# Linear attention and channel mix on one core: q turned in blocks on VectorE, the attention weights moved by DMA, and an order from a table

## The chip, the core and the metric

The kernel runs on one core of one Trainium2 chip. TensorE (PE) multiplies matrices, VectorE (DVE), ScalarE (ACT) and GpSimd (POOL) do elementwise work, and SyncE (SP), ACT and POOL issue DMA transfers. The metric is the device time of one execution in microseconds, the median of several.

## What is computed

Inputs in float32: q, k and v of (8 batches, 8 heads, 576 rows, 64), and the weights of a feed-forward part. The reference, cut to what matters:

```python
def _attn_ref(q, k, v):
    q_s = softmax(q, over the 64 columns)
    k_s = softmax(k, over the 576 rows)
    kv = einsum('bhsd,bhse->bhde', k_s, v)
    return einsum('bhsd,bhde->bhse', q_s, kv)

def _moe_ref(x, mu_k, mu_r, w_k, w_v, w_r):      # x: (8, 576, 512), heads side by side
    x_prev = x shifted by one row, zeros first
    xk = mu_k * x + (1.0 - mu_k) * x_prev
    xr = mu_r * x + (1.0 - mu_r) * x_prev
    k = np.maximum(xk @ w_k, 0.0)                # (512, 1024)
    v = k * k @ w_v                              # (1024, 512)
    r = 1.0 / (1.0 + np.exp(-(xr @ w_r)))        # (512, 512)
    return r * v
```

There is no softmax over a square matrix: each head's k and v give a 64 x 64 matrix kv, and q is multiplied by it.

## The kernel before

**Attention.** `attention(b, g)` handles four heads of one batch: g is 0 or 1. Their q, k and v are loaded as float32 into `raw` buffers of 128 partitions: a partition holds nine rows of a head, and two heads lie one above the other. ACT takes the exponent of q and of k to bfloat16 (`eq`, `ek`, L423) and casts v (`vv`, L430). DVE sums q's rows (`rsum`, L437), inverts the sums (L440) and scales (`qs`, L445). PE transposes `qs` against an identity in nine 128 x 128 blocks into the PSUM tile `att` (L472), and ACT copies the result to `qt` (L476). PE forms kv in 18 products on 64 rows each (L453), one column of ones in `vv` giving the sums over k's rows as well. DVE inverts these (`rz`, L460) and scales kv into block-diagonal weights `w` (L560). PE multiplies them with `qt` (x, L566), ACT copies the product to `xb` (L571), and DVE mixes each row with the row before: `edge` (L575), `diff` (L579), a product with mu (L584) and a sum (L589) into `xk` and `xr`, which hold four batches. Batch 0 goes another way: its weights are multiplied with mu beforehand (`mu_mask`, L513), so that PE does the mixing as well (L525), and its results are copied to `xk` and `xr` (L530).

**Channel mix.** `unit(half, c0, n)` handles 512 or 256 columns of `xk` and `xr`: eight groups of four products with `wk_bf` (L646), a relu on ACT (`rel`, L631), a square on DVE (`k2`, L635); then, per 128 rows, four products with `wr_bf` (L677), a tanh on ACT (L682), eight products with `wv_bf` (L687), the gate on DVE (`ot`, L693) and two stores of 128 KB on SP's queue (L703).

**Order.** Every step is entered with `plan.add`, with its engine, an assumed duration, what it depends on and which buffers it takes. `Plan.order` then plays the program through: `set_due` gives each step a due time, counted back from the channel mix, and of the steps that could start on an engine the one with the least due time is taken. `early` and `AHEAD` shift due times. The result is a fixed order for each engine; an engine executes its own strictly in that order. `pools` gives the number of buffers of each kind. The tiles `mm` (four of one PSUM bank) and `att` (two of two banks) fill PSUM.

**Loads.** Batch 0's q, k and v come in halves on ACT's and SP's queues (`FIRST`). All else goes by POOL's queue: the weights, cast to bfloat16 by the transfer, in the order wk, wr, wv, with batch 1's loads between and behind (`SOON`), then the batches 2 to 7. The first weight load waits for one of batch 0's loads (`GATE`).

Of the kernel before, what the change touches and what calls it, by code (L numbers as in the profile page):

```python
# [19 lines left out]
SPARE = 0  # L20
LOOK = {"PE": 0.03, "ACT": 0.2, "DVE": 0.1, "POOL": 0.03, "SP": 0.03}
AHEAD = (1.0, 4, 8)
# [8 lines left out]
         (0, 2, ("SP", "SP")), (1, 1, ("SP", "SP")), (1, 2, ("SP", "SP")))  # L31
ORDER = (0, 1, 2)
SOON = {(1, 0, 0): 2.2, (1, 0, 1): 2.4, (1, 1, 0): 2.7, (1, 0, 2): 3.5}
GATE = 6
FILL = 0
ON_PE = (0,)
CASTS = (("ACT", "ACT"), ("ACT", "ACT"))
EVAC = ((("ACT", "DVE"), ("ACT", "ACT")), (("ACT", "DVE"), ("ACT", "ACT")))

# [10 lines left out]
class Op:  # L50


    def __init__(self, engine, occ, lat, key, emit, deps, takes, gives, size):
        self.engine, self.occ, self.lat, self.key = engine, occ, lat, key
        self.emit, self.deps, self.takes, self.size = emit, list(deps), list(takes), size
        self.start = self.end = None
        self.early = 0.0
        for slot in gives:
            slot.last.append(self)


class Plan:
# [11 lines left out]
    def add(self, engine, occ, lat, key, emit, deps=(), takes=(), gives=(), size=0.0):  # L74
        op = Op(engine, occ, lat, key, emit, [d for d in deps if d is not None], takes, gives,
                size)
        self.ops.append(op)
        return op

    def slot_time(self, slot):  # L80
        best = None
        for i, parts in enumerate(self.pools[slot.pool]):
            free = 0.0
            for user in (self.user.get(part) for part in parts):
                if user is not None:
                    late = [o.end for o in user.last]
                    free = None if not late or None in late or free is None else max(
                        [free] + late)
            if free is not None and (best is None or free < best[0]):
                best = (free, i)  # L90
        return best
# [9 lines left out]
    def set_due(self):  # L101
        after = {}
        for op in self.ops:
            for d in op.deps:
                after.setdefault(d, []).append(op)
        seen = set()
        for root in self.ops:
            stack = [(root, False)]
            while stack:
                op, closed = stack.pop()  # L110
                if closed and not op.size:
                    for o in after.get(op, ()):
                        op.key = min(op.key, o.key - op.lat - HOP - SPARE)
                    op.key -= op.early
                elif op not in seen:
                    seen.add(op)
                    stack.append((op, True))
                    stack += [(o, False) for o in after.get(op, ())]

    def order(self):  # L120
        self.set_due()
# [3 lines left out]
        waiting = {}  # L125
        for op in self.ops:
            waiting.setdefault(op.engine, []).append(op)
        done = []
        left = len(self.ops)
        while left:  # L130
            chosen = None
            for engine, ops in waiting.items():
                now = free.get(engine, START)
                ready = None
                for op in ops:
                    if any(d.end is None for d in op.deps):
                        continue
                    t = max([now] + [d.end + HOP for d in op.deps])
                    ok = True
                    for slot in op.takes:  # L140
                        got = self.slot_time(slot)
                        if got is None:
                            ok = False
                            break
                        t = max(t, got[0] + HOP)
                    if not ok:
                        continue
                    rank = (max(t, now + LOOK[engine]), op.key)
                    if ready is None or rank < ready[0]:
                        ready = (rank, t, op)  # L150
                if ready is not None and (chosen is None or ready[1] < chosen[1]):
                    chosen = ready
            assert chosen is not None, "no operation can start"
            _, t, op = chosen
            for slot in op.takes:
                slot.index = self.slot_time(slot)[1]
                for part in self.pools[slot.pool][slot.index]:
                    self.user[part] = slot
# [12 lines left out]
            waiting[op.engine].remove(op)  # L171
            done.append(op)
            left -= 1
        return sorted(done, key=lambda o: o.start)
# [3 lines left out]
def kernel(  # L178
# [25 lines left out]
    pools = {"raw": 12, "eq": 3, "ek": 2, "vv": 2, "stat": 4, "qs": 2, "qt": 3, "w": 3, "wp": 4,  # L204
             "rz": 3, "xb": 2, "xd": 2, "xm": 3, "k2": 2, "rel": 3, "th": 2, "ot": 3, "mm": 4,
             "att": 2, "early": 2}
    shared = {("early", i): [("mm", 2 * i), ("mm", 2 * i + 1)] for i in range(2)}
    plan = Plan(pools, shared)
# [17 lines left out]
    ws = buffers("w", [128, 2, 128], BF16)  # L226
    wps = buffers("wp", [128, 2, 2, 128], BF16)
    rzs = buffers("rz", [128, 2], F32)
    xbs = buffers("xb", [128, 2, 64 + S], BF16)
    xds = buffers("xd", [128, 2, S], BF16)  # L230
    xms = buffers("xm", [128, 2, S], BF16)
    k2s = buffers("k2", [128, FT, 512], BF16)
    rels = buffers("rel", [128, 512], BF16)
# [14 lines left out]
    wk_bf = const.tile([128, CT, F], BF16, name="wk_bf")  # L248
# [9 lines left out]
    mu_mask = const.tile([128, 2, 2, CT, 128], F32, name="mu_mask")  # L258
# [6 lines left out]

    def load(engines, b, g, i, key, deps=()):
        slot = Slot("raw")
        src = (q, k, v)[i]
        us = PARTS[len(engines)]

        def emit(engine, u):
            ap = bass.AP(tensor=src.tensor,
                         offset=src.offset + (b * H + 2 * g + 4 * u.start) * S * D,
                         ap=[[J * D, 128], [4 * S * D, u.stop - u.start], [1, J * D]])
            return queues[engine].dma_start(out=raws[slot.index][:, u, :], in_=ap)

        ops = [plan.add(e, 0.71 if e == "POOL" else 0.45, 0.5, key + 0.1 * n,
                        lambda e=e, u=u: emit(e, u), deps, [slot] if n == 0 else [],
                        size=590.0 / len(engines))
               for n, (e, u) in enumerate(zip(engines, us))]  # L280
        loaded[b, g, i] = (ops, slot)
        return ops

    first = []
    for n, (g, i, engines) in enumerate(FIRST):
        first += load(engines, 0, g, i, n)

# [20 lines left out]

    def emit_mask_zeros():
        nc.vector.memset(mu_mask[:].rearrange("p m s c e -> p (m s c e)"), 0.0)  # L310

    def emit_late_consts():
        for t in ws:
            nc.vector.memset(t[:].rearrange("p a b -> p (a b)"), 0.0)
        for t in xbs:
            nc.vector.memset(t[:, :, 0:1], 0.0)

# [4 lines left out]
    consts = plan.add("DVE", 0.2, 0.3, -9, emit_consts, [identity])  # L322
    late_consts = plan.add("DVE", 0.6, 0.7, LATE, emit_late_consts)
    mask_zeros = plan.add("DVE", 1.8, 1.9, 0, emit_mask_zeros)
# [47 lines left out]
    def weight_part(dst, src, n, u, c0, c1):  # L372
        ap = bass.AP(tensor=src.tensor, offset=src.offset + (4 * u + c0) * D * n,
                     ap=[[n, 64], [D * n, c1 - c0], [1, n]])
        return nc.gpsimd.dma_start(out=dst[64 * u:64 * u + 64, c0:c1, :], in_=ap)

    gate = [first[GATE]]
    sync = mybir.DependencyInfo(mybir.DependencyClass.Sync, mybir.DependencyReason.DATA)

    def emit_wk(h):  # L380
        for u in range(2):
            ld = weight_part(wk_bf, moe_w_k, F, u, 2 * h, 2 * h + 2)
            if h == u == 0:
                tc.add_manual_dep(ld.ins, gate[0].made.ins.name, sync)

    wk_done, wv_done = [], []
    for h in range(2):
        wk_done.append(plan.add(
            "POOL", 1.25, 1.25, h, lambda h=h: emit_wk(h), gate, size=1048.0))
    wr_done = plan.add("POOL", 1.25, 1.25, 2, lambda: [  # L390
        weight_part(wr_bf, moe_w_r, C, u, 0, CT) for u in range(2)], gate, size=1048.0)

    def emit_wv(h):
# [3 lines left out]
        nc.gpsimd.dma_start(out=wv_bf[:, h * n:(h + 1) * n, :], in_=ap)  # L397

    for h in range(2):
        wv_done.append(plan.add("POOL", 0.75, 0.75, 3 + h, lambda h=h: emit_wv(h), gate,  # L400
                                size=1048.0))
    for b in range(1, B):
        for g in range(2):
            for n, i in enumerate(ORDER):
                load(["POOL"] * (2 if b == 1 else 1), b, g, i,
                     SOON.get((b, g, i), 100 * b + 10 * g + n), gate)
# [6 lines left out]
    def attention(b, g):  # L413
# [14 lines left out]
        def cast_v(copy, u):  # L428
            to = vvs[vv.index][:, :, 0:128].rearrange("p j (u d) -> p j u d", u=2)
# [340 lines left out]
```

## Time and profile before

| what | us |
|---|---|
| three executions | 211.36, 211.47, 212.88 |
| median | 211.47 |
| span of the profiled execution | 210.3 |
| PE, DVE, ACT, POOL busy in it | 192.2, 160.3, 150.9, 43.2 |
| moved by DMA in it | 40.62 MB |

The profile is of one execution. A line such as `L646 PE MATMUL mm_c<-xk,wk_bf` names the kernel's line, the engine, the operation, and the tile written with the tiles read. In an answer on waits a line reads: who waited, for whom, microseconds in all, times, the longest. In the chain of waits a line has the start, the microseconds and the work. For transfers, a line has the target and source, the issuing queue, their number, the size of each and the median time in us from issue to landing. The bytes counted are those written, so a weight load that casts counts half of what it reads.

### The profile page before, as it was taken

The page shows a single profiled execution, that of the slowest core. Times are in us where ns is not written, and L with a number is a line of the kernel's source. Part 1 is how long each engine was busy: PE and PEld are TensorE (multiplying, and loading weights), DVE is VectorE, ACT ScalarE, POOL GpSimd, SP SyncE. Part 2 cuts the span into 40 slices and gives each one's busy share as a digit, 9 for nine tenths or more (in the row PEclk, how much of TensorE's full clock was granted, in tenths as well). Part 3 has the DMA queues.
Part 4 walks back from the last instruction along what each step waited for, and adds up shares of the span by engine and source line. Part 5 has one row for each costly group of instructions (what it writes and reads, how often), then busy time and mean ns, then how long its engine had stood idle before and what let it go on. Part 6 is the DMA issues. An engine that isn't in the chain of part 4 may idle for free.

```text
span 210.3 us, 3597 instructions
## 1 busy us (share of the span) xinstructions
PE 192.2 (91%) x1283; PEld 97.2 (46%) x1283; DVE 160.3 (76%) x364; ACT 150.9 (72%) x229; POOL 43.2 (21%) x72
## 2 busy tenths in 40 slices
PE   3089998967999999999999999999999999999991
PEld 0065444433544544445467444445444554444740
DVE  6488684999999999999959995957796469632531
ACT  5596798998999999759599977338964862452440
POOL 3793656534334132301100000000000000000000
PEclk9999999999999999999999999999999999999999
DMA  6999999999999999983871130350034003502424
GB/s 216 367 215 201 346 267 394 392 405 403 392 395 404 404 383 339 317 277 112 245 196 41 31 69 0 71 119 14 6 86 111 2 3 85 115 0 50 102 51 100
DMA packets 15898, 40.62 MB, mean 193 GB/s; under 512 B 2300, under 2 KB 3848, under 8 KB 15880
## 3 DMA queue, kind: packets, MB, share of 16 engines
q0 software_dynamic: 8384, 27.40, 39.7%
q1 hardware_dynamic: 7064, 12.10, 20.4%
q10 hardware_dynamic: 432, 0.88, 1.3%
q8 instruction: 10, 0.16, 0.3%
q14 instruction: 8, 0.07, 0.1%
HBM read 33.56 MB, written 9.44 MB: 204 GB/s over the span
## 4 chain that ended last, share of the span: by engine, by line
PE 82%; DVE 7%; ACT 4%; DMA 3%; issue 1%; ACTq 0%; DVEq 0%
PE mm_b L646 9%; PE mm_c L646 8%; PE mm_a L687 7%; PE mm_d L687 7%; PE mm_b L687 7%; PE mm_a L646 6%; PE mm_c L687 6%; PE mm_d L677 5%; PE mm_d L646 5%; PE mm_c L677 4%; DMA raw_b<-in_k_dram 3%; PE mm_a L677 2%; PE att_a L472 2%; PE att_a L453 2%; PE att_b L453 2%; PE att_b L472 2%
## 5 line engine op out<-in xcount | busy, mean ns | idle before, releaser
L646 PEld LDWEIGHTS <-wk_bf 128*128 128x128 bf16 x320 | 30.4, 98 | 31.0 <-issue 2.3
L646 PE MATMUL mm_b<-xk,wk_bf 128*128 128x512 bf16 (+1 forms) x96 | 23.2, 357 | 0.0
L646 PE MATMUL mm_c<-xk,wk_bf 128*128 128x512 bf16 (+1 forms) x92 | 22.6, 361 | 0.0
L677 PEld LDWEIGHTS <-xr 128*128 128x128 bf16 x144 | 13.4, 98 | 16.0 <-issue 0.7
L687 PEld LDWEIGHTS <-k_a 128*128 128x128 bf16 x144 | 13.5, 98 | 15.8 <-issue 0.5
L687 PEld LDWEIGHTS <-k_b 128*128 128x128 bf16 x144 | 13.4, 98 | 15.7
L646 PE MATMUL mm_a<-xk,wk_bf 128*128 128x512 bf16 (+1 forms) x72 | 17.1, 355 | 0.0
L646 PE MATMUL mm_d<-xk,wk_bf 128*128 128x512 bf16 (+1 forms) x60 | 14.9, 358 | 1.6 <-DVE xk L589 1.6
L677 PE MATMUL mm_d<-wr_bf,xr 128*128 128x512 bf16 x56 | 14.4, 379 | 0.0
L687 PE MATMUL mm_a<-wv_bf,k_a 128*128 128x512 bf16 x48 | 12.3, 379 | 0.0
L682 ACT ACTIVATE th_a<-mm_d 128x512 f32<-128x512 f32 x12 | 7.2, 602 | 6.8 <-PE mm_d L677 6.6
L677 PE MATMUL mm_c<-wr_bf,xr 128*128 128x512 bf16 x40 | 10.3, 379 | 0.1
L687 PE MATMUL mm_d<-wv_bf,k_a 128*128 128x512 bf16 x40 | 10.3, 379 | 0.0
L687 PE MATMUL mm_c<-wv_bf,k_b 128*128 128x512 bf16 x40 | 10.3, 379 | 0.0
L687 PE MATMUL mm_b<-wv_bf,k_b 128*128 128x512 bf16 x40 | 10.1, 379 | 0.0
L472 PEld LDWEIGHTS <-qs_a 128*128 128x128 bf16 x72 | 4.9, 103 | 8.6 <-DVE qs_a L445 7.4
L635 DVE TENSOR_TENSOR k_a<-rel_a 128x512 bf16<-128x512 bf16 (+1 forms) x13 | 5.1, 391 | 4.6 <-ACT rel_a L631 4.5
L631 ACT ACTIVATE rel_a<-mm_b 128x512 bf16<-128x512 f32 (+1 forms) x10 | 5.4, 539 | 4.0 <-PE mm_b L646 3.8
L687 PE MATMUL mm_a<-wv_bf,k_b 128*128 128x512 bf16 x32 | 8.2, 379 | 0.0
L687 PE MATMUL mm_d<-wv_bf,k_b 128*128 128x512 bf16 x32 | 8.2, 379 | 0.0
L687 PE MATMUL mm_c<-wv_bf,k_a 128*128 128x512 bf16 x32 | 8.2, 379 | 0.0
L682 ACT ACTIVATE th_b<-mm_a 128x512 f32<-128x512 f32 x6 | 3.6, 594 | 6.3 <-PE mm_a L677 6.3
(258 smaller groups left out, 452.5 us busy)
## 6 DMA issues: line engine op xcount, KB each, us to landing
out_dram<-ot_a SPq DMA_DIRECT2D x24, 128.0 KB, 2.7
out_dram<-ot_b SPq DMA_DIRECT2D x24, 128.0 KB, 2.4
out_dram<-ot_c SPq DMA_DIRECT2D x24, 128.0 KB, 2.7
raw_a<-in_q_dram POOLq DMA_DIRECT2D x3, 576.0 KB, 10.3
raw_c<-in_k_dram POOLq DMA_DIRECT2D x2, 576.0 KB, 10.3
raw_b<-in_v_dram POOLq DMA_DIRECT2D x2, 576.0 KB, 10.5
raw_d<-in_q_dram POOLq DMA_DIRECT2D x2, 576.0 KB, 10.2
raw_e<-in_k_dram POOLq DMA_DIRECT2D x2, 576.0 KB, 10.9
```

What stands on the lines that cost most here:

```text
L453: nc.tensor.matmul(kv_of(kvp, hf)[:, 0:129], lhsT=eks[ek.index][r, j, :, :].rearrange("p u d -> p (u d)"), rhs=vvs[vv.index][r, j, 0:129], ...
L472: nc.tensor.transpose(out=transposed()[:, j, :], in_=qss[qs.index][:, j, :], identity=ident[:])
L631: nc.scalar.activation(out=rels[rel.index][:, 0:n], in_=bank(kf)[:, 0:n], func=ACT.Relu, scale=HALF_ROOT)
L635: nc.vector.tensor_tensor(out=k2s[k2.index][:, fc, 0:n], in0=rels[rel.index][:, 0:n], in1=rels[rel.index][:, 0:n], op=ALU.mult)
L646: nc.tensor.matmul(bank(kf)[:, 0:n], lhsT=wk_bf[:, ct, fc * 128:(fc + 1) * 128], rhs=xs[0][:, ct, c0:c0 + n], start=(ct == 0), stop=(ct == ...
L677: nc.tensor.matmul(bank(rps), lhsT=xs[1][:, ct, c:c + 128], rhs=wr_bf[:, ct, :], start=(ct == 0), stop=(ct == CT - 1))
L682: nc.scalar.activation(out=ths[th.index][:], in_=bank(rps), func=ACT.Tanh, scale=0.5)
L687: nc.tensor.matmul(bank(vps), lhsT=k2s[k2.index][:, ft, 128 * m:128 * m + 128], rhs=wv_bf[:, ft, :], start=(ft == 0), stop=(ft == FT - 1))
```

## The change

Six things change.

1. Batches 2 to 7 go through a new function, `batch(b)`, which handles all eight heads at once. q is loaded in another layout (two transfers of 64 partitions for four heads), its exponent, sums and scaling are as before, and `turn_q` then transposes it on DVE in blocks of 32 x 32, taking two bfloat16 as one 4-byte element; PE's transposes and ACT's copies of them are gone. Since an element is a pair of columns, the 64 columns of a head come apart into 32 pairs: k's exponent writes its columns in the same order, and x is the sum of two products, r = 0 and 1.
2. kv of both groups goes into one `att` tile. Its inverse sums and weights are formed once per batch, without the block-diagonal zeros (`wn`), and four transfers on SP's queue move them from SBUF to SBUF into `w`, where each head has its 32 partitions.
3. x then is sixteen products per half batch, on tiles of 32 rows and 64 columns, 288 moving columns each, into two `att` tiles.
4. Batch 0's v is cast by its load, on POOL's queue, into the first `k2` buffer; its ACT casts are gone. `mu_mask` lies in the other `k2` buffer.
5. `wk_bf` becomes two tiles by columns, and the loads' order changes: batch 1's k and v, then parts of wk, q, wr and wv. `held` lets the first of POOL's gated loads wait, whichever it is.
6. The order is no longer found by due times: `ORDER_OF` lists all steps. `early`, `AHEAD` and `set_due` are gone. Some pools grow (`ek`, `vv`, `xb` to 3, `qt` and `rel` to 4).

The stores of batches 2 to 7 write rows in the new order. The core of the diff:

```diff
 FIRST = ((0, 0, ("ACT", "ACT")), (1, 0, ("SP", "SP")), (0, 1, ("ACT", "SP")),
-         (0, 2, ("SP", "SP")), (1, 1, ("SP", "SP")), (1, 2, ("SP", "SP")))
+         (1, 1, ("SP", "SP")), (0, 2, ("POOL",)), (1, 2, ("POOL",)))
...
-GATE = 6
+GATE = 5
...
+ORDER_OF = (
+    0, 20, 8, 16, 1, 10, 17, 13, 11, 3, 12, 6, 5, 2, 4, 14, 9, 15, 7, 21, 78, 79, 22, 80, 24, 81,
...
     def order(self):
-        self.set_due()
...
+        for i in ORDER_OF:
+            op = self.ops[i]
...
+    def batch(b):
...
+            def turn_q(qs=qs, qt=qt):
+
+                nc.vector.transpose(
+                    out=qts[qt.index][:].rearrange("p j c -> p (j c)").bitcast(F32),
+                    in_=qss[qs.index][:].rearrange("p j c -> p (j c)").bitcast(F32))
...
+                for y in range(u.start, u.stop):
+                    nc.scalar.activation(
+                        out=eks[ek.index][:].rearrange("p j u d -> p j (u d)").rearrange(
+                            "p j (r y d) -> p j y d r", r=2, y=2)[:, :, y, :, :],
+                        in_=raws[sk.index][:, y, :].rearrange("p (j d r) -> p j d r", d=32, r=2),
+                        func=ACT.Exp)
...
+        def kv():
+            for g in range(2):
+                for j in range(J):
+                    for x in range(2):
+                        r = slice(64 * x, 64 * x + 64)
+                        nc.tensor.matmul(
+                            bank(kvp)[:, x, 256 * g:256 * g + 129],
+                            lhsT=eks[eks_[g].index][r, j, :, :].rearrange("p u d -> p (u d)"),
+                            rhs=vvs[vvs_[g].index][r, j, 0:129], start=(j == 0),
+                            stop=(j == J - 1), skip_group_check=True)
...
+        def weights(x):
+            nc.vector.tensor_tensor(
+                out=wns[wn.index][:, x, :, :], in0=by_group(0, 128)[:, x, :, :],
+                in1=rzs[rz.index][:, 2 * x:2 * x + 2, None].to_broadcast((128, 2, 128)),
+                op=ALU.mult)
+
+        def move(x):
+            for r in range(2):
+                nc.sync.dma_start(out=ws[w.index][64 * x:64 * x + 64, r, :, :],
+                                  in_=wns[wn.index][64 * r:64 * r + 64, x, :, :])
...
+            def x(h=h, xps=xps):
+                for r in range(2):
+                    for a in (0, 2, 1, 3):
+                        q = slice(32 * a, 32 * a + 32)
+                        y, hi = a % 2, a // 2
+                        for g in range(2):
+                            turned = qts[qts_[g].index][:].rearrange(
+                                "p j c -> p (j c)").rearrange("p (t r) -> p t r", r=2)
+                            nc.tensor.matmul(
+                                bank(xps[y])[64 * g:64 * g + 64, hi, 0:32 * J],
+                                lhsT=ws[w.index][q, r, g, 64 * y:64 * y + 64],
+                                rhs=turned[q, 32 * J * h:32 * J * h + 32 * J, r],
+                                start=(r == 0), stop=(r == 1), skip_group_check=True)
...
     for b in range(B):
-        for g in range(2):
-            attention(b, g)
+        if b < BY_GROUP:
+            for g in range(2):
+                attention(b, g)
+        else:
+            batch(b)
```

## The prediction

> **What bounds the kernel now.** I read the page's head first (busy shares), then its slices, then the waits of PE, then the chain of waits in order of time, then the queue's transfers in three stretches.
>
> The head and three rows of the slices (40 equal parts of the span, 5.26 us each):
>
> ```profile
> span 210.3 us, 3597 instructions
> ...
> PE 192.2 (91%) x1283; PEld 97.2 (46%) x1283; DVE 160.3 (76%) x364; ACT 150.9 (72%) x229; POOL 43.2 (21%) x72
> ...
> PE   3089998967999999999999999999999999999991
> ...
> DVE  6488684999999999999959995957796469632531
> ...
> DMA  6999999999999999983871130350034003502424
> ```
>
> PE has 18.1 us without work, all at the two ends and in slices 6 to 9; the DMA engines are full until about 84 us; DVE is full from 43 to 100 us. What PE waited for, largest first:
>
> ```profile
> PE att_a L472 <- DVE qs_a L445: 5.7, 2, 5.5
> PE mm_a L340 <- DMA mu_rows<-in_moe_mu_r_dram: 3.5, 1, 3.5
> PE mm_d L646 <- DVE xk L589: 1.6, 1, 1.6
> PE att_b L453 <- ACT vv_a L430: 1.4, 2, 1.2
> PE att_a L472 <- DVE qs_b L445: 0.6, 1, 0.6
> ```
>
> The two largest lie before 11.1 us. The others make up nearly all of PE's 3.7 us of gaps between 33 and 48.5 us (0.57, 0.15, 1.21, 0.15, 1.62 in PE's timeline). After 48.48 us the chain is PE alone up to 205.6 us, then the last product with the gate and its store. A piece of it (start, us, what):
>
> ```profile
> 72.29 0.86 PE mm_d L646 x4
> 73.15 0.63 PE att_b L453 x18
> 73.78 0.97 PE mm_c L646 x4
> 74.75 0.63 PE att_a L453 x18
> 75.39 0.97 PE mm_b L646 x4
> 76.36 0.86 PE mm_d L677 x4
> ```
>
> So from 48 us on, only fewer PE microseconds, or a new wait of PE, can move the end. Four 512-column products take 0.86 us, and 0.97 after each kv product (18 products on 64-row tiles): a change of tile shape costs 0.11. One of a kv product's 18 takes 0.63/18 = 35 ns although 129 columns last 0.86/4 x 129/512 = 54 ns: the two row tiles overlap.
>
> **The change, part by part.** Sums are made against this execution (210.3 us, 1.2 below the median of 211.47); I apply their differences to the median.
>
> *PE work of batches 2 to 7.* Removed: twelve transposes of nine, 0.50 each (53.00 to 53.50 in the chain) = 6.0. kv: before 12 x (0.63 + 0.11) = 8.9; after, both groups stand in a row, 6 x (36 x 0.035 + 0.11) = 8.2. x: before 12 x (0.24 + 0.25) = 5.9; after, 12 halves of 16 products on 32-row tiles, 64 columns of weights, 288 moving columns. No row shows such tiles. From below: eight at a time, two rounds of 288 columns (0.121) = 0.24. From above: all serial, 16 x 0.121 = 1.94. I take the pace of the nearest tiles, 16 x 35 ns = 0.56, as it is the pace at which load and product pairs go by there, and 0.11 for the change of shape: 12 x 0.67 = 8.0. Sum: -6.0 - 0.7 + 2.1 = **-4.6**; at the ends -8.4 and +12; if no more than two tiles overlap (0.97 a half) +0.4.
>
> The row is the 0.97: every x is now also a change of shape, which x was not before. [...]
>
> *The gaps between 33 and 48.5 us.* Before, batch 1's last load is issued at 27.6 us behind wk, wr and half of wv, and lands 9.1 us later, near 36.7. After, POOL's queue holds six of batch 1's twelve loads ahead of wk, three more ahead of wk's second half, the last ahead of wr. Bytes read until then: 3.54 MB (batch 0) + 3.54 + 2.10 = 9.2 MB; by the moved bytes of the stretches (weights read at twice what is written) about 8.6 MB are in by 25 us and 11 by 30, so batch 1 is complete near 26.5, ten us earlier. DVE, 35% idle between 20 and 40 us, can take its work then, and in the new order batch 1's mixing stands ahead of batch 2's row sums (which put 2.9 us between 43.2 and 46.1 before xd_b). wr and wv slip to about 28.5, 30.5 and 33; r and v come at about 29, 32 and 34. Tight, so of 3.7 I take **-3.0** (bounds -3.7 and -1).
>
> *The start.* Batch 0's v by a casting load takes four casts of 0.6 = 2.3 us (10.63 to 11.9, 14.44 to 15.6) from ACT, which had no gap between 8.3 and 12; the first x could come up to 2 us sooner. But the loads are the limit: wk's first part stands behind 3.54 + 1.77 MB, 6.36 MB with itself, and 6.35 MB are read by 20 us. The first k product, 18.82 before, then starts near 20, with two more x (2 x 0.5) done by then. Net **0**; bounds -1.5 and +1.5. The v loads on POOL go ahead of the identity (0.7 us on POOL; the 0.74 us rows of POOL's issues), which the mu rows' product waits for; mu_wide and the masks slip by as much and were needed only at 13.9, four us after they were done.
>
> *DVE, ACT.* Per batch DVE gets two block transposes and loses 2 x (0.58 + 0.16) of weights and reciprocals for 2 x 0.42 + 0.17 (0.29 for 128 columns; the gate's 512 take 0.69, so 128 more cost 0.13; 1.0 in all). A transpose: no row; 576 four-byte elements, between 0.36 (L584's 576) and 1.35 (L445's 1152); I take 0.67, the half of the 1.35, for half as many elements at L445's pace. Net +0.9 a batch, 5 in all, on an engine full until 100 us. At nothing, since PE never waits for it after 48.5 and DVE has 32 us idle after 100; without that cover it is 3 batches x 0.9 = 2.6. [...] ACT loses two copies of 1.13 a batch and gets k's exponent in two halves (2 x 0.68 for 1.18): -1.9 a batch, hidden.
>
> *The new wait: kv to x goes through a DMA.* Each batch's weights now travel SBUF to SBUF: four transfers on SP's queue (1.11 us of issue per pair), between the stores of the output. x stands in PE's order with all later products queued behind it. A store of 128 KB lands thus:
>
> ```profile
> out_dram<-ot_b SPq DMA_DIRECT2D x4, 128.0 KB, 5.8
> ...
> out_dram<-ot_b SPq DMA_DIRECT2D x13, 128.0 KB, 2.4
> ```
>
> The first is the stretch 60 to 85 us with full DMA engines (30 to 60 us: 7.3 to 8.3), the second 120 us to the end. The moves have as many rows (64) and a quarter of the bytes. In the order of the changed program PE has between kv and x: batch 2, 6.0 us of products; batches 3 and 4, 6.9; batches 5 to 7, eight groups or more at emptier DMA. From kv's end to the last landing: batch 2, reciprocal 0.1, weights 0.4, a square 0.4, a row sum 1.3, weights 0.4, first issue 0.6 = 3.2 and the landing; batch 3, a gate 0.6 and its store's issue ahead, 3.5 and the landing. With 2.4: 5.6 and 5.9, covered. With 5.8: waits of 3.0 and 2.4. With 8.3: 5.5 and 4.9. Batch 4 by the 85 to 120 us stretch (2.4 to 4.5): 0 to 0.4. I take 4.0 for these small transfers, between the ends: 1.2 + 0.6 = **+1.8**; bounds 0 and +11.
>
> Sum: -4.6 - 3.0 + 0 + 1.8 = -5.8; 211.5 - 5.8 = **205.7**. What is left alone: all of the feed-forward products, the last unit and the store at the end.
>
> **Rivals.**
> *Late moves (slower).* Place: x of batches 2, 3 and 4. If a small transfer waits as long behind the loads as the slow stores do, 7.5 to 8.3 for three batches, PE stands 5 + 4.5 + 3.5 = 13 us: 211.5 - 7.6 + 13 = 217. It decides against the change from 2.5 us a batch on. For it: the DMA row is full until 84 us, and batches 2 and 3 lie at 45 and 62. Against: the 5.8, and that a stall lets the loads run on.
> *Two tiles at a time.* x at 0.97 a half: gain only from the gaps, 211.5 - 3.0 + 1.8 + 0.4 = 210.7. For it: only two-fold overlap is shown.
> *DVE becomes the bound.* Block transposes at 1.35, +2.3 a batch over three batches, PE waits for squares: 205.7 + 6.8 = 212.5.
> *All covered.* Moves land in time, x at 0.35: 211.5 - 8.4 - 3.0 = 200.
>
> **Numbers.** Forecast 0.55, all covered 0.11, two tiles 0.11, DVE 0.07, late moves 0.16 (half of it under 214). About 1% is what a measurement here can tell from no change. Faster than 209.4: 0.55 + 0.11 and a little of the two-tile case, 0.67; slower than 213.6: most of the late moves and some of DVE, 0.17; between, 0.16. The range takes the forecast with x between 0.35 and 0.9 and moves up to 6 us, and reaches to the two-tile and DVE cases: 200.5 to 212.5.
>
> **What would show it.** PE busy near 187 of the span; the sixteen products of one x in 0.5 to 0.7 us; no wait of PE for DVE between 30 and 50 us; PE's waits for w's transfers under 2 us in sum; DVE's block transpose near 0.7. A wait of x of over 2.5 us in each of batches 2 to 4, or x over 1 us, makes it wrong.

## The result and the profile after

The changed kernel takes 327.94 us (median; 326.11 to 331.92) against 212.1 for the kernel before on the same chip: 1.543 times as long, 95% interval 1.533 to 1.553. Ratios here and below leave out executions in a slower state (one of the four, 331.92), medians do not. The forecast was 205.7.

The page of the changed kernel; the rows of the slices are parts of 8.1 us here.

```profile
span 324.3 us, 3678 instructions
...
PE 209.1 (64%) x1296; PEld 96.4 (30%) x1319; DVE 165.7 (51%) x361; ACT 184.8 (57%) x225; POOL 53.3 (16%) x86
...
PE   2588893167675398749850969767994919985000
...
PEclk9999999589799789997995679996996966997555
DMA  8999999999999614670552110110010011011111
GB/s 241 299 247 244 276 216 248 160 314 296 230 238 204 181 27 111 171 204 4 159 132 78 64 51 26 60 51 36 32 59 24 27 47 53 4 34 51 51 51 39
DMA packets 28485, 40.85 MB, mean 126 GB/s; under 512 B 12840, under 2 KB 17460, under 8 KB 28468
...
DMA 42%; PE 15%; ACT 14%; DVE 13%; issue 6%; POOL 2%; SPq 2%; DVEq 0%; ACTq 0%; POOLq 0%
```

PE was busy 91% of the span before and led the chain of waits; now it is at 64% and the chain is led by DMA. ACT has 34 us of work more where 11 us less were expected. The last three slices have no work of PE at all. From the 23rd slice on the GB/s row never passes 64, and at the end, without any other work, it stands at 51, as if at a ceiling. The bytes are the same (40.85 MB, 40.62 before), but 12,840 packets are under 512 bytes; before, 2,300 were.

That ceiling in four stretches of the changed kernel (busy us of PE, PEld, DVE, ACT and POOL, with the number of instructions; then the granted clock, the mean share of the 16 DMA engines, and GB/s):

```profile
180.00:220.00 40.00, 32.38 (x186) 13.65 (x187) 26.15 (x52) 30.57 (x34) 0.00 (x0) 0.88 0.15 51
220.00:260.00 40.00, 33.27 (x214) 13.86 (x217) 24.85 (x53) 18.92 (x27) 0.00 (x0) 0.85 0.11 35
260.00:300.00 40.00, 29.08 (x126) 14.01 (x127) 11.78 (x28) 11.00 (x22) 0.00 (x0) 0.83 0.11 38
...
300.00:324.00 24.00, 0.00 (x0) 0.00 (x0) 1.38 (x2) 0.00 (x0) 0.00 (x0) 0.50 0.12 48
```

In the last stretch only stores of the output run, at a share of 0.12, as much as about two of sixteen engines would give (0.12 x 16 = 1.9). From 180 to 300 us there are only stores and the moves of kv weights, at 0.11 to 0.15. Who waits for them, on DVE and then on PE:

```profile
DVE ot_b L915 <- DMA out_dram<-ot_b: 16.3, 4, 6.6
DVE ot_a L915 <- DMA out_dram<-ot_a: 15.3, 2, 10.8
...
DVE ot_c L915 <- DMA out_dram<-ot_c: 13.3, 4, 5.0
```

```profile
PE mm_a L868 <- DVE ot_a L915: 10.8, 1, 10.8
PE att_a L779 <- DMA w_b<-wn_a: 10.3, 4, 4.1
```

The gate cannot write `ot` because its last contents have not been stored (45 us of DVE's waiting); the gate holds a PSUM bank, so PE waits for the gate. And the moves, issued on SP's queue between the stores, land late. From the chain (start, us, what):

```profile
97.98 13.55 DMA w_b<-wn_a
...
136.51 9.54 DMA w_a<-wn_a
...
165.23 17.99 DMA out_dram<-ot_c
```

ACT's extra work has one line, k's exponent:

```profile
L700 ACT ACTIVATE ek_a<-raw_i 128x576 bf16<-128x576 f32 x4 | 10.8, 2967 | 0.0
```

2.91 to 3.06 us in the rows of this line, where the prediction had 0.68 by batch 1's exponent of the same size. With 24 of these an estimate is 24 x 2.3 = 55 us of ACT.

### The profile page after: what moved, and what is told of

Read it like the earlier page. It is cut to its first block, busy times and chain, and to the rows that moved or that the text cites. A ratio compares the mean times of both kernels' runs of the same rounds, so it can differ in the third digit from the quotient of the medians.

```text
span 324.3 us, 3678 instructions
## 1 busy us (share of the span) xinstructions
PE 209.1 (64%) x1296; PEld 96.4 (30%) x1319; DVE 165.7 (51%) x361; ACT 184.8 (57%) x225; POOL 53.3 (16%) x86
## 2 busy tenths in 40 slices
DMA packets 28485, 40.85 MB, mean 126 GB/s; under 512 B 12840, under 2 KB 17460, under 8 KB 28468
## 4 chain that ended last, share of the span: by engine, by line
DMA 42%; PE 15%; ACT 14%; DVE 13%; issue 6%; POOL 2%; SPq 2%; DVEq 0%; ACTq 0%; POOLq 0%
DMA out_dram<-ot_c 12%; DMA out_dram<-ot_b 9%; DMA w_b<-wn_a 7%; DMA raw_a<-in_q_dram 5%; ACT ek_c L700 4%; ACT ek_a L700 4%; DMA raw_j<-in_v_dram 3%; DMA w_a<-wn_a 3%; DMA wk_a<-in_moe_w_k_dram 2%; PE mm_b L909 2%; PE mm_d L868 2%; DVE k_b L857 2%; PE mm_c L868 1%; PE mm_c L909 1%; PE mm_d L909 1%
## 5 line engine op out<-in xcount | busy, mean ns | idle before, releaser
L868 PEld LDWEIGHTS <-wk_b 128*128 128x128 bf16 x160 | 16.5, 104 | 41.4 <-issue 25.5
L868 PEld LDWEIGHTS <-wk_a 128*128 128x128 bf16 x160 | 16.1, 103 | 24.9 <-issue 11.0
L868 PE MATMUL mm_a<-xk,wk_b 128*128 128x512 bf16 (+1 forms) x36 | 10.3, 413 | 15.5 <-DVE ot_a L915 10.8
L899 PE MATMUL mm_c<-wr_bf,xr 128*128 128x512 bf16 x35 | 10.9, 434 | 9.4 <-ACT th_a L904 3.2
L899 PE MATMUL mm_a<-wr_bf,xr 128*128 128x512 bf16 x47 | 14.0, 420 | 3.0 <-ACT rel_b L853 2.7
L909 PE MATMUL mm_b<-wv_bf,k_a 128*128 128x512 bf16 x46 | 13.4, 417 | 2.4 <-DVE ot_b L915 2.1
L868 PE MATMUL mm_c<-xk,wk_b 128*128 128x512 bf16 (+1 forms) x40 | 10.4, 372 | 4.7 <-ACT th_a L904 3.2
L909 PE MATMUL mm_d<-wv_bf,k_b 128*128 128x512 bf16 x47 | 13.1, 400 | 0.1
L868 PE MATMUL mm_b<-xk,wk_b 128*128 128x512 bf16 (+1 forms) x46 | 12.3, 386 | 0.1
L868 PE MATMUL mm_c<-xk,wk_a 128*128 128x512 bf16 (+1 forms) x40 | 11.1, 394 | 1.8 <-DVE ot_b L915 1.6
L700 ACT ACTIVATE ek_a<-raw_i 128x576 bf16<-128x576 f32 x4 | 10.8, 2967 | 0.0
L868 PE MATMUL mm_a<-xk,wk_a 128*128 128x512 bf16 (+1 forms) x38 | 10.1, 374 | 0.1
## 6 DMA issues: line engine op xcount, KB each, us to landing
raw_b<-in_k_dram POOLq DMA_DIRECT2D x2, 576.0 KB, 16.2
```

The lines of the kernel that those rows point to most:

```text
L700: nc.scalar.activation(out=eks[ek.index][:].rearrange("p j u d -> p j (u d)").rearrange("p j (r y d) -> p j y d r", r=2, y=2)[:, :, y, :, ...
L868: nc.tensor.matmul(bank(kf)[:, 0:n], lhsT=wk_bf[fc // 4][:, ct, fc % 4 * 128:fc % 4 * 128 + 128], rhs=xs[0][:, ct, c0:c0 + n], start=(ct = ...
L899: nc.tensor.matmul(bank(rps), lhsT=xs[1][:, ct, c:c + 128], rhs=wr_bf[:, ct, :], start=(ct == 0), stop=(ct == CT - 1))
L909: nc.tensor.matmul(bank(vps), lhsT=k2s[k2.index][:, ft, 128 * m:128 * m + 128], rhs=wv_bf[:, ft, :], start=(ft == 0), stop=(ft == FT - 1))
```

## The experiments

Three theories came out of these lines. **S**: the stores of batches 2 to 7, whose pattern in DRAM now has an outermost dimension of 2 (2 x 32 rows), are the bound. **E**: k's exponent is, through the order in which it writes. **Q**: q's loads are, cut into small packets. First each by itself. The runs were made on several chips, on which the kernel before took 212.0 to 213.4 us; each ratio is against it on the same chip, and a difference of about 1 us between runs of different chips means little.

**Stores alone.** Each 64-row store of batches 2 to 7 as two of 32 rows, without the outer 2:

```diff
-ap = [[C, 2], [2 * J * C, 32], [1, C]]           # one store of 64 rows
+ap = [[2 * J * C, 32], [1, C]]                   # two stores, offsets j and j + 1
```

> Each store of 64 rows of batches 2 to 7 becomes two of 32 rows, so that its outer dimension is 32 and not 2. Theory S (these stores go over 2 of the 16 DMA engines: the profile shows a DMA share of 0.10 to 0.12 at 51 GB/s from 180 us to the end, and moves of w landing 10 to 13 us after their issue behind them): the stretch at 51 GB/s is gone, stores land in 2 to 4 us after 150 us, w in under 5, time 240 to 275. Theory E (the exponent of k sets the time, 24 x 2.95 us on ACT): the stores matter only at the end, 300 to 315. Theory O (the fixed order and the wait for moved weights as such): over 300, PE's waits for w about as before.

271.1 us (one execution): 57 less. The transfer lines of this run show the same data without a queue:

```profile
out_dram<-ot_c SPq DMA_DIRECT2D x44, 64.0 KB, 1.7
```

The median landing of the moves falls to 3.7 us for one buffer of `w` and 6.9 for the other. S holds, but is not all.

**Exponent alone.** The same elements to the same places; only the order of the walk differs, so that 32 neighbours of the result come one after the other, and the reads, not the writes, take every second element:

```diff
-out "p j (r y d) -> p j y d r",  in "p (j d r) -> p j d r"
+out "p j (r y d) -> p j y r d",  in "p (j d r) -> p j r d"
```

> k's exponent walks its elements in another order: 32 neighbours of the result innermost, where the changed kernel alternates between two places 64 elements apart; the values and their places are the same. Theory E: an exponent of 576 falls from 2.95 to about 0.7 us, ACT's busy time from 185 to about 130, time under 260. Theory S: the exponent falls as well, but 7.1 MB of stores at 51 GB/s are 139 us, the first of them near 80 to 120 us: 250 to 300, DVE still waits for ot's stores.

```profile
L700 ACT ACTIVATE ek_a<-raw_i 128x576 bf16<-128x576 f32 x4 | 2.7, 720 | 0.0
```

A quarter of the time per operation, and ACT is busy 139.4 us; the whole is at 312.4, 15 us less, with the 51 GB/s and the waits for stores still there. That is above the ranges of both theories, and E as the main bound falls. The edit also made the reads take every second element, so it is the writing that was slow; whether by the distance or by changing place at every element, no run separates.

**q's loads with shorter rows.** Each load of 4608-byte rows as two of 2304:

```diff
-ap=[[2 * S * D, 2], [2 * J * D, 32], [1, 2 * J * D]]
+ap=[[2 * S * D, 2], [2 * J * D, 32], [1, J * D]]      # twice, by columns
```

> The loads of q of batches 2 to 7 are cut by columns, rows of 2304 bytes in place of 4608, twice as many transfers. Theory Q (rows of 4608 bytes are sent in packets under 512 bytes: 12840 such packets against 2300 before, and a rate of 230 against 393 GB/s between 30 and 60 us): packets under 512 bytes fall to about 2500, the rate from 30 to 60 us rises to 350 or more, time 5 to 25 us less, 300 to 320. If the outer dimension of 2 is what slows these loads, nothing changes. Theories S and E: time changes by less than 10 us.

319.2 us (one execution, 8.8 less). From 30 to 60 us 3,018 of 5,848 packets are under 512 bytes, at 229 GB/s; in the changed kernel 3,208 of 5,904, at 236. The row's length isn't what cuts the packets; the outer dimension of 2 was left.

**The three together.**

> All three edits together. If S, E and Q are the whole of it: 200 to 207 us, under the kernel before, PE busy near 186, PE's only later waits those for w in batches 2 to 4, under 5 us in sum. Theory O (order, waits for moved weights, DVE's block transposes): over 215.

249.9 us, ratio 1.172 (1.161 to 1.183). A miss: 14,844 small packets remain, and q's loads of batches 2 to 7, cut in two, land in a median 7.6 to 16.2 us at half the bytes. So two more forms of q's load, both with stores and exponent mended: four loads of 32 partitions, one for each head; and one load of 128 partitions in the order of memory, which leaves the heads exchanged.

```diff
+ap=[[2 * J * D, 32], [1, 2 * J * D]]             # four loads, one head each
+ap=[[2 * J * D, 128], [1, 2 * J * D]]            # or one, four heads
```

> Stores in 32-row pieces and k's exponent with 32 neighbours innermost, as in the run that joined three edits, and q of batches 2-7 loaded one head at a time: 32 partitions of 4608 bytes, no outer dimension of 2 in the pattern. Theory O (the outer dimension of 2 makes the q loads slow and cuts them into pieces of 512 bytes): the packets under 512 bytes fall from 14844 to near the 2300 of the kernel before, the DMA rate at 30-60 us rises from 215 GB/s towards the 390 of before, the q loads land in 3-7 us, and the time is 200-212 us. Theory P (a transfer over only 32 or 64 partitions is slow whatever its pattern): the packets may change, but the rate at 30-60 us stays near 215 GB/s and the time stays at 240-255 us.

> As the run beside it, but q of batches 2-7 comes with one load of 128 partitions of 4608 bytes in memory order, so two of each four heads' q stand in exchanged places and the output is not the reference's; all sizes, waits and places are the same. Theory O: time 198-210 us, small packets near 2300, and little apart from the run with four loads of 32 partitions. Theory P: this run is far faster than the one with loads of 32 partitions (which stays at 240-255): 198-210 against 240-255. If both stay at 240-255, q's loads aren't what is left, and the moves of the kv weights behind the stores on one queue are the next suspect.

225.0 us (ratio 1.053, 1.047 to 1.060) and 219.3 (1.028, 1.020 to 1.035). The stretch 40 to 50 us, in the changed kernel, with four loads of 32 partitions, and with one of 128:

```profile
40.00:50.00 10.00, 9.20 (x41) 3.96 (x41) 6.29 (x14) 3.89 (x5) 2.24 (x4) 1.00 1.01 232
```

```profile
40.00:50.00 10.00, 9.93 (x45) 4.38 (x45) 7.50 (x15) 6.49 (x10) 4.49 (x8) 1.00 1.01 292
```

```profile
40.00:50.00 10.00, 9.94 (x49) 4.29 (x49) 8.72 (x17) 8.35 (x12) 4.28 (x7) 1.00 1.03 400
```

The engines' share is 1.0 in all three, at 232, 292 and 400 GB/s: here a full share says nothing of the rate. Without the outer 2 the small packets fall to 4,092 and 3,516 and the time by 25 us (theory O, the outer dimension), though neither theory's range was met. With the outer 2 the rows also went from 2304 bytes back to 4608; the run with shorter rows alone speaks against these as the cause. But the rate is back at 400 GB/s only over 128 partitions, so P has a part, 5.7 us. The next kernel shows that part from the other side: q in one load, and k and v paired to it by two loads of 64 partitions each.

> The run with one q load of 128 partitions, made whole: k and v of batches 2-7 are loaded in two pieces of 64 partitions so that each 32-row tile has the head that the memory's order of q gives it, and x writes its two banks accordingly. All of the reference is computed. Both theories: 216-222 us, as with one q load, and small packets near 3500. If loads over 64 partitions were slow by themselves, 235 or more.

230.9 us (1.081, 1.075 to 1.088), 11.6 more than with k and v over 128 partitions. It lies between the two cases, nearer to loads that are slow by themselves:

```profile
40.00:50.00 10.00, 9.33 (x42) 4.07 (x42) 6.99 (x12) 5.92 (x9) 4.12 (x7) 1.00 1.03 237
```

**The moves.** In the run at 219.3 us PE still waits for kv weights:

```profile
PE att_a L776 <- DMA w_b<-wn_a: 3.9, 2, 2.7
...
PE att_b L776 <- DMA w_a<-wn_a: 3.3, 4, 1.8
```

and one such wait costs more than itself (stretches of 2 us; the clock is the last but two):

```profile
78.00:80.00 2.00, 2.00 (x11) 0.88 (x9) 2.00 (x5) 1.47 (x3) 0.00 (x0) 1.00 1.05 413
80.00:82.00 2.00, 0.42 (x2) 0.00 (x0) 1.19 (x3) 0.79 (x2) 0.00 (x0) 1.00 0.62 217
82.00:84.00 2.00, 0.31 (x2) 0.10 (x2) 0.00 (x0) 0.00 (x0) 0.00 (x0) 0.87 0.09 33
84.00:86.00 2.00, 1.38 (x16) 0.56 (x17) 0.00 (x0) 0.65 (x2) 0.00 (x0) 0.50 0.03 9
86.00:88.00 2.00, 1.78 (x5) 0.76 (x5) 0.00 (x0) 1.13 (x2) 0.00 (x0) 0.50 0.00 0
88.00:90.00 2.00, 2.00 (x20) 0.48 (x19) 0.00 (x0) 0.48 (x1) 0.00 (x0) 0.50 0.00 0
90.00:92.00 2.00, 2.00 (x10) 0.82 (x8) 1.77 (x6) 0.70 (x2) 0.00 (x0) 0.92 0.00 0
```

PE stands for about 4 of the 6 us from 80 to 86, and from 84 on the granted clock is 0.50 for 6 us. PE is busy 5.2 of these; at half the clock an estimate of 2.6 us is lost on top of the wait. After another wait the clock is 0.50 from 61 to 65 us, and 0.65 in the two us before and behind. So the next kernel issues the moves but reads the weights where DVE left them:

```diff
-lhsT=ws[w.index][q, r, g, 64 * y:64 * y + 64]
+lhsT=wns[wn.index][q, r, g, 64 * y:64 * y + 64]
```

> The run with one q load of 128 partitions (219.3 us), and x reads the kv weights where VectorE left them, not where the moves put them; the moves are still issued, but nothing waits for them. The halves stand in the wrong rows, so x, and the output, are not the reference's; all sizes are the same. Theory D (late moves): in the run at 219.3 us TensorE waited 3.9 + 3.3 = 7.2 us for moves, and the granted clock was at 0.5 for about 6 us after each of the two long stalls (59-66 and 80-90 us), which loses another 5 us or so; both go, and the time is 204-210 us. Theory R (what is left is the loads' rate or the order of the work, and the moves only cover it): other waits take their place and the time stays at 215-220.

208.6 us (0.981, 0.976 to 0.985): 10.7 us less (10.0 by the ratios), and the clock is 0.99 on average. D holds. The kernels from here on compute the whole reference. First x was moved later, in the kernel with k and v over 64 partitions:

> As the run beside it, and x of batches 2 and 3 moved later on TensorE, behind four more groups of the second stage's matmuls (0.86 us each, 3.4 us in all); nothing else of the order changes but the evictions that read x. Theory D: the waits for moves in batches 2 and 3 (nearly 7 us) go and the clock stays granted there: 208-213 us, level with or below the kernel before. Theory R: 216-222, the same as without it. A third case: the later x makes the mixes late, and TensorE waits for xk instead: above 219.

232.8 us against 230.9 (ratios 1.080 and 1.081): no gain. PE still waited 9.5 us for moves, 13.1 before, so this didn't decide. Next, k's columns in the order (y, r, d): with that, half of the weights already lie on the rows where x reads them, and the other half must go 32 partitions further. First DVE writes it there, straight out of PSUM.

```diff
+for y in range(2):
+    to, at = 64 * y + 32 * x, 64 * y + 32 - 32 * x
+    nc.vector.tensor_tensor(out=ws[w.index][to:to + 32, :, :],
+        in0=by_group(0, 128)[at:at + 32, x, :, :], in1=..., op=ALU.mult)
```

> Stores in 32-row pieces, k's exponent with 32 neighbours innermost, q in one load of 128 partitions, and no moves: k's columns stand in the order (y, r, d), half of the kv weights is read where it lies, and the other half is written 32 partitions further by VectorE itself, straight out of PSUM (4 operations of 32x256 a batch more, 12 DMAs of 32 KB and their places on the queue of SP fewer). All of the reference is computed. Theory D: as the run without a wait for the moves (208.6 us), give or take the 4 operations (some 0.3 us each, 7 us of VectorE in all, beside TensorE): 204-210, below the kernel before. Theory R: VectorE, now busier, holds up TensorE: 211-217.

217.6 us (1.025, 1.016 to 1.034). R, just above its range: DVE is busy 175.0 us, and 10.9 more from 10 us on than in the run at 208.6 (167.0 for 156.1). Over the 24 operations that makes an estimate of 0.45 us each, about as long as the full 128 rows (0.33 to 0.43). PE waits for transposes, squares, mixes and gates in many places. This kernel also has a second `wn` buffer, as have those after it. It served as a base to put back one defect at a time; k's exponent there alternates between places 32 elements apart, not 64.

> The run beside it with the stores of the changed kernel put back (an outer dimension of 2 over 32 rows). Theory S (the stores are a bound of their own, at some 51 GB/s): 7.1 MB take 139 us; from the first such store near 95 us that gives 230-250. If they cost only by what stood behind them on the queue of SP (the moves, which are gone here): 204-215.

> The run beside it with the order in which the changed kernel writes k's exponent put back (neighbours 32 apart): 24 operations of 2.95 us for 0.72, 54 us of ScalarE more, all of it before 150 us or so. Theory E (ScalarE becomes the bound of batches 2-7): 220-240. If it is covered, as the prediction had it: 204-212.

265.2 and 259.4 us (one execution each): +47.6 for the stores, +41.8 for the exponent. Both are bounds of their own, and both ran above their ranges. That mending the exponent alone brought only 15 would fit if in the changed kernel each hid much of the other; no run mends just these two. Then the 24 operations as copies on ScalarE:

> The run at 217.6 us, with the 24 writes of kv weights 32 partitions further taken from VectorE and made by ScalarE as copies of 32x256 out of the tile that VectorE has written. All of the reference is computed. If VectorE is what holds the run at 217.6 (busy 175.0 us, 9.97 of the 10 us at 60-70, 19.8 of the 20 us at 140-160): it is busy 165 us again, and the time is 206-211, as where x doesn't wait for the moves (208.6), and below the kernel before. If not: 214-219. A third case: the copies stand in ScalarE's order ahead of evictions and wait there for VectorE, which gives 209-214.

214.1 us (1.006, 1.002 to 1.011): DVE is busy 157.6 us from 10 us on, 9.4 less (0.39 for each of the 24), and 3.5 us are won, on the border between the third case and the second; a copy takes 0.40 us. Where x waits for nothing, PE works 59.4 us of the 60 from 120 to 180; here 57.1. Last, the copies for batches 2 and 3 alone and DMAs for batches 4 to 7, and, beside it, DMAs for all with x of batches 2 and 3 four places later:

> The run at 214.1 us, with ScalarE's copies kept for batches 2 and 3 alone; in batches 4-7 the same 32-row blocks are moved by 4 DMAs of 16 KB on the queue of SP. All of the reference is computed. With one q load of 128 partitions the waits for moves lay at 58-61 and 80-85 us (batches 2 and 3) and only 0.5 us later, so these DMAs should be covered; TensorE lost 2.3 us more at 120-180 us in the run at 214.1 than where x waits for nothing. If the operations are the price: 211-213, within 1% of the kernel before or just below it. If not: 214 or more.

> The run beside it with no copies on ScalarE at all: 4 DMAs of 16 KB in every batch, and x of batches 2 and 3 moved four places later on TensorE (3.4 us). All of the reference is computed. Theory D (late moves, and nothing else, are left once the patterns and the exponent are mended): the waits of 7 us go without a cost on another engine, 208-212, below the kernel before by up to 2%. If x's later place costs as much as the wait: 213-217.

**210.4 us, ratio 0.989 (0.984 to 0.994)**, 1.1% below the kernel before and far below the changed one; and 215.2 (1.010, 1.006 to 1.014). The later x loses as much as the wait: its waits for moves are down to 0.6 us, but PE then works 7.2 of the 10 us from 60 to 70 and DVE 3.9 of those from 80 to 90. The page of the fastest whole kernel, and one x in PE's timeline:

```profile
span 208.4 us, 3721 instructions
...
PE 184.5 (89%) x1296; PEld 90.1 (43%) x1319; DVE 164.2 (79%) x361; ACT 140.9 (68%) x233; POOL 43.2 (21%) x74
...
PE   2268878999878999999999999999999999999990
...
PEclk9999999999999999999999999999999999999999
```

```profile
107.54 0.81 PE L910 MATMUL mm_a<-wv_bf,k_b 128*128 128x512 bf16 x3
108.50 0.31 PE L779 MATMUL att_a<-qt_a,wn_a 32*64 32x288 bf16 x1
...
108.52 0.31 PE L779 MATMUL att_b<-qt_b,w_a 32*64 32x288 bf16 x1
108.65 0.28 PE L779 MATMUL att_a<-qt_a,w_a 32*64 32x288 bf16 x1
...
108.89 1.04 PE L900 MATMUL mm_d<-wr_bf,xr 128*128 128x512 bf16 x4
```

Eight products start within 0.02 us, eight more 0.15 later, and the next work 0.39 after the first. The four products before x (one record is missing) are due to end at 108.40, by 0.86 for four, so x takes 0.10 + 0.39 = 0.49 with the change of tile shape.

## Why the prediction was wrong

The mechanism it was about, fewer PE microseconds against a new wait, was right in sign once the rest was mended; it failed on steps that it priced at nothing, or by rows that didn't fit. The first three make 109 of the 122 us that it missed by: with them mended, in the run with q's heads exchanged, the time is 219.3.

1. **"What is left alone: ... the store at the end."** The prediction has no term for the stores of batches 2 to 7, whose pattern changed from 64 rows to 2 x 32, and it priced the moves behind them by the old stores' landing. The new stores run at 51 GB/s: 57 us by mending them alone, 47.6 by putting them back where no move stands behind them. With nothing but stores the share is 0.12, near 2/16, and the pattern's outermost dimension is 2. That this dimension sets how many engines work is the author's estimate; no trace here shows which engines a store uses.
2. **"k's exponent in two halves (2 x 0.68 for 1.18): -1.9 a batch, hidden."** The row taken, 128x576, fits in size but not in the order of writing. Alternating between two places 128 bytes apart costs 2.95 us; the same elements in runs of 32 cost 0.72. Put back in the mended kernel, with places 64 bytes apart, it makes ACT busy 46.6 us more from 10 us on (179.9 for 133.2), 1.9 for each of the 24, and costs 41.8 in all: not hidden.
3. **q's loads, at nothing.** Their layout was told in the change and costed nowhere. Against one load of 128 partitions the outer 2 and the fewer partitions cost 249.9 - 219.3 = 30.6 us, 24.9 of it gone with the outer 2. With k and v loaded over 64 partitions the rate from 40 to 50 us was 237 GB/s, over 128 it was 400, and q came over 128 in both; what limits the narrower loads is not shown. Why an outer 2 on POOL's queue shows as small packets at a full share, and not as two engines, these runs leave open.
4. **The new wait, +1.8, "I take 4.0 for these small transfers".** In the run at 219.3 us x's last wait for a move ends 5.9 us after the last issue in batch 2 (55.16 to 61.02) and 6.4 after it in batch 3 (78.18 to 84.62). With these for landings the prediction's own sum gives an estimate of 3.1 + 3.0 = 6.1 us of waiting, and the trace has 7.2 over all batches. The whole cost was 10.7, within the bounds of 0 and 11 and near the 13 of the late-moves rival; what no step had is the halved clock after the waits.
5. **PE work, -4.6.** In the fastest kernel PE is busy 184.5 for 192.2: -7.7. The tiles overlap eight at a time (eight start within 0.02 us), and x takes 0.49 for the 0.67 of the prediction; the lower end (-8.4) was nearer. Two tiles at a time is refuted.
6. **The gaps, -3.0.** Between 30 and 50 us PE works 19.1 of 20 us in the fastest kernel, 18.0 in the run at 208.6, and 16.3 before: 1.7 to 2.8 won, within the bounds.
7. **The start, 0 (bounds 1.5).** The first k product starts at 22.4 to 22.9 us in the changed kernel, the runs at 219.3 and 208.6 and the fastest, not near 20. In the first 30 us PE does 17.7 to 19.7 us of work there for 20.4, so 0.7 to 2.7 are lost. This takes back much of the gaps.
8. **DVE's transposes, "At nothing".** 0.77 us for 0.67. The cover was thin: PE works 26.4 of the 30 us from 50 to 80 in the fastest kernel, where before it worked all 30; and 10.9 us more of DVE's work cost 9 (208.6 to 217.6). That the transposes cause the 3.6 us is argued, not shown.

With steps 1 to 3 mended and nothing waiting for the moves 208.6 is left. The forecast without its 1.8 for that wait is 203.9, so 4.7 remain (3.5 by the ratio). In that run's profile PE is busy 8.5 us less than before, but without work 5.0 us more, where 3.0 less were forecast: +1.9 in the first 30 us, -1.7 from 30 to 50, +2.6 from 50 to 80 and +2.2 behind.

## What to carry to other kernels

When a change alters a layout, list every access pattern that it touches, the stores and loads "left alone" too, and price each by a row with the same outermost dimension and number of partitions, not by bytes. For an elementwise operation, find a row with the same order of writing, not only the same size. And price a wait of PE with the slower clock that may follow it (here 0.50 for about 6 us).

## What was not expected of the hardware

- A pattern of 2 x 32 rows runs at 51 GB/s on SP's queue; on POOL's queue the same outer 2 keeps the engines' share at 1.0, at 232 GB/s, with some 11,000 more packets under 512 bytes (14,844 against 3,516 to 4,092).
- After PE stood for about 4 of 6 us, and another time for 2.8 of 6, the granted clock was 0.50 for about 6 us.
- An exponent that wrote alternately to two places 128 bytes apart took 2.9 to 3.1 us; the same elements written in runs of 32 took 0.72 to 0.75. With the places 64 bytes apart ACT was busy 46.6 us more over 24 of them.
- An operation on 32 partitions whose result lies 32 partitions further took an estimated 0.39 to 0.45 us on DVE and a measured 0.40 on ACT for 256 elements, beside 0.33 to 0.43 on DVE for 128 partitions in place.
